# A two-layer kernel on one core: group 0 of the second up stage as seven products, its weight words made during the first stage, and down 1 in another order of products

## The chip, the core and the metric

The kernel runs on one core of a Trainium2 chip. A core has a matrix engine (TensorE, PE in the profile), a vector engine (VectorE, DVE), a scalar engine (ScalarE, ACT), GpSimd (POOL) and a queue engine (SyncE, SP), which issues all the DMAs of this kernel. Matmuls write PSUM, eight banks of 512 fp32 columns by 128 partitions; DVE and ACT read and write PSUM and SBUF. The metric is the device time of one execution in microseconds (us), lower is better. It is compared by medians of several runs.

## What is computed

Attention over small windows (4 batches, 8 heads of 64, 768 positions, chunks of 32 queries) gives x, 3072 tokens by 512. Two feed-forward layers follow, all in fp32:

```
x = attention(q, k, v, mem_k, mem_v)         # 3072 x 512
h = x @ moe_w_in                             # 512 x 2048
g = s * max(h, 0)**2 + b
x = g @ moe_w_out                            # 2048 x 512
h = x @ moe2_w_in
g = h - tanh(h)
out = g @ moe2_w_out
```

## The kernel before

**Four stages.** Up 1 (0 to 350.7 us; attention and h of layer 1), down 1 (to 579.9), up 2 (to 819.8), down 2 (to 1052.0). Tokens are the matmuls' columns, 512 a time. Six blocks of 512 tokens make three groups g of 1024. Each fp32 product is three matmuls of reduced operands (`three`, L154 to 157): each operand is split into a high part, copied by ACT, and a low part, the difference, on DVE. The weights come from DRAM as 64-bit words; a 1024-wide piece is rebuilt by ACT (`scaled`, L162) and DVE (`shifted`, L168, and `filled`, L172).

**Seven products.** Both down stages take the 2 x 2 blocks of a matrix product as seven products P1 to P7 of combined blocks instead of eight. The up stages store for each strip of h the seven combinations of its quadrants (`combine`, L443) in DRAM (`o1`, `o2`), and a down stage (class `Down`, L453) loads them as parts. It runs seven passes, one for each product in the order of `ORDER`, of 12 entries (three groups by two halves by two), 12 matmuls an entry. `split(i + 2)` makes the high and low parts two entries ahead of `multiply(i)`. When a group's product is complete, `final1` (L684) adds it to running sums. In down 1 the results are the quadrants X, U, V, Q of the new x, and for groups 1 and 2 also their combinations T1 to T4.

**Up 2.** Eight column strips n of w_in. Group 0 is a plain product: `plain_column` (L948), 12 matmuls, four a strip. Groups 1 and 2 are a `Quad` (L966): seven products of six matmuls in the order P1, P7, P6, P2, P5, P3, P4, the first product of a quad ahead of the end of the one before. ACT copies the running bank out after P1, P6 and P5 (`copy`, L988), DVE adds a second bank (`add`, L991), ACT takes tanh (L995), DVE subtracts (`curve`, through `minus`, L673) and makes the combinations, SP stores them. The strip's weights are rebuilt, split, combined and split again in between (`w2_*`, L793 to 841).

**What sets the order.** The program's order is written out by hand: each engine runs its own instructions in the order in which the code emits them. In up 1 a list of tokens (`START`) orders the first two blocks, then a loop emits each tile t of a block j (L762 to 788): the attention step, the products, `up1_relu` on ACT, `up1_square` on DVE, and at a strip's end the combinations. The attention step (`att_step`, L353) stands on every fourth tile: ACT copies the transposed weights (L314), then `x_high` (L347), later the exponentials (L291). During down 1 the entries carry steps from tables: `WEIGHTS` makes the pass's weights, `READY` loads, scales and fills the w_out words of layer 2 and stores them in DRAM (`wz`), `SUMS` and `SPLITS` make the T operands.

Of the kernel before, what the change touches and what calls it, by code (L numbers as in the profile page):

```python
# [8 lines left out]
F32 = mybir.dt.float32  # L9
# [35 lines left out]
R10 Q14 R11 E10 F18 V9 st2 k3 F17 D10 Q16 X9 K3 r18 T10 r17 Q17 E11 Q18 F19 vv11 r19 C10 Q19 F21 F20  # L45
D11 r20 st3 L9 r21 Q20 V10 k4 K4 T11 X10 F23 F22 L10 r23 Q21 C11 V11 X11 L11 F24 r22 st4 Q23 R12 Q22
vv12 F26 r24 F25 r26 Q24 F27 r25 Q26 k5 K5 Q25 F28 F29 r27 Q27 r28 F30 k6 st5 K6 E12 st6 Q28 r29 F31
# [3 lines left out]
WEIGHTS = {  # L51
# [7 lines left out]
for q in (2, 5, 6):  # L59
    for h in range(2):  # L60
        WEIGHTS[q - 1, 4 * h] = [("sums", q, h), ("high", q, h)]
        WEIGHTS[q - 1, 4 * h + 1] = [("low", q, h)]

READY = {
    (0, 0): [("load", 0, "E7")], (0, 3): [("scale", 0, "E14"), ("load", 1, "E13")], 
    (0, 6): [("fill", 0)], (0, 7): [("load", 2, "E7")], (0, 9): [("scale", 1, "E15")], 
    (1, 0): [("fill", 1)], (1, 1): [("load", 3, "E13")], (1, 2): [("scale", 2, "E14")], 
    (1, 6): [("fill", 2)], (1, 7): [("load", 4, "E7")], (1, 8): [("scale", 3, "E15")], 
    (1, 10): [("fill", 3)], (2, 1): [("scale", 4, "E14")], (2, 10): [("fill", 4)],
    (3, 0): [("load", 5, "E7")], (3, 4): [("scale", 5, "Z9")],  # L70
    (3, 8): [("fill", 5), ("load", 6, "E7")], (4, 2): [("scale", 6, "Z0")],
    (4, 5): [("fill", 6), ("load", 7, "E7")], (4, 8): [("scale", 7, "Z1")],
    (4, 11): [("fill", 7)],
}

SUMS = {(4, 9): [("T3", 1)], (5, 0): [("T3", 2)], (5, 9): [("T1", 1)], (5, 10): [("T2", 1)],
        (6, 1): [("T1", 2)], (6, 2): [("T2", 2)]}

SPLITS = {(5, 6): [("T3", 1)], (6, 5): [("T1", 1)], (6, 9): [("T4", 1)], (6, 10): [("T3", 2)], (6, 11): [("T1", 2)]}

ORDER = ("P1", "P6", "P5", "P7", "P3", "P2", "P4")
# [3 lines left out]
SLOT = {"P1": 0, "P3": 1, "P2": 2, "P5": 3, "P6": 4, "P7": 5, "P4": 6}  # L85


@with_exitstack
def tile_chunk_attention_two_ffn(
# [30 lines left out]
    SIZE = {"E": 2048, "Z": 1024, "Y": 1024, "Q": 1280, "S": 768, "R": 512}  # L120
# [55 lines left out]
    def filled_in_raw(z, raw):  # L176
# [8 lines left out]
    A_RAW = ("E8", "E9")  # L185
    A_QK, A_V = ("Q0", "Q1", "Q2"), ("Z0", "Z1", "Z2")
# [6 lines left out]
    B_S = (("Z2", "Z3"), ("Z4", "Z6"))  # L193
# [3 lines left out]
    B_ACC = {"X": ("Y0", "Y1", "Y2"), "U": ("Y3", "Y4", "Y5"), "V": ("E6", "E6", "Z7")}  # L197
    X2 = {"Q": ("E13", "E14", "E15"), "V": ("E16",),
          "X": (("Z9", "Z10"), ("Z2", "Z3"), ("Z4", "Z6")), "U": ("E7", "E6", ("Z0", "Z1"))}
    B_TMP = ("E16", "E17", "Z8")  # L200
    C_RAW, C_Z, C_W = "E0", "Z5", ("E1", "E10")
    C_OT = (("E4", "E5"), ("E8", "E12"))
    C_T = {("T3", 1): ("Z11", "Y0"), ("T1", 1): "E2", ("T2", 1): "E3", ("T4", 1): "E17",
           ("T3", 2): "E11", ("T1", 2): "E9", ("T2", 2): ("Z8", "Y1"), ("T4", 2): ("Z7", "Y2")}
    C_SHL, C_SNAP = ("Y3", "Y4"), "Y5"
    C_SHL7 = "E0"
    Z2 = {("A11", 0): "Y3", ("A11", 1): "Y4", ("A21", 0): "Z11", ("A21", 1): "Z2",
          ("A22", 0): "Z3", ("A22", 1): "Z8", ("A12", 0): ("E0", 0), ("A12", 1): ("E0", 1)}
    D_WHL = (("E14", "E6"), ("E13", "E16"))
    D_STREAM = ("E1", "E17", "E2", "E9", "E7")  # L210
    D_RING = ("E3", "E11", "E15")
    D_S = (("Z4", "Z6"), ("Z0", "Z1"))
    D_ACC = {"X": ("Z7", "Z5", "Z9"), "U": ("Y0", "Y1", "Y2"), "V": ("E4", "E4", "E12")}
    D_OUT = ("E5", "E8")
# [11 lines left out]
    def make_masks():  # L226
        for nm in ("mid", "first", "last"):
            m = const.tile([P, KE], F32, name=f"mask_{nm}")
# [224 lines left out]
    class Down:  # L453


        def __init__(self, src, zmap, smap, whl, stream, ring, load, view, pick, bias, final, turn, ahead, first):
# [3 lines left out]
            self.later, self.end = [], None  # L460
            self.loaded, self.turn, self.ahead = 0, turn, ahead
            self.parts = [(p, g, h) for p in range(7) for g in (range(NG) if p else first) for h in range(2)]
# [22 lines left out]
        def place_z(self, key):  # L485
            place = self.zmap[key]
            if isinstance(place, tuple):
                if place[1] == 0:
                    self.zt[place[0]] = new(place[0], 2048, F32, "zq")
# [11 lines left out]
        def load_part(self, i):  # L501
            p, g, h = self.parts[i]
            self.part[i] = new(self.stream[i % len(self.stream)], 4 * NB, F32, "part")
            self.load(self.part[i], ORDER[p], g, h)
# [12 lines left out]
        def sums(self, p, half):  # L517

            z = lambda k: self.z[k, half]
            name = ORDER[p]  # L520
# [42 lines left out]
        def split(self, i):  # L563
# [6 lines left out]
            if self.bias is not None and ORDER[p] in ("P1", "P2", "P3", "P6"):  # L570
# [678 lines left out]
```

## Time and profile before

| | us |
|---|---|
| median of 3 runs (lowest, highest) | 1053.42 (1053.35, 1054.23) |
| the profiled execution | 1053.9 |
| its span | 1052.0 |
| PE busy in the span | 1035.1 |
| DVE, ACT busy | 799.4, 529.1 |
| DMA moved | 250.55 MB, 238 GB/s |

The profile is one execution seen by the hardware profiler. A busy time is the sum of an engine's instructions; a matmul's record is longer than the distance to the next one, because they overlap in the pipeline, so that PE's price of a matmul is the distance of two starts. A wait is the idle time before an instruction, put down to the instruction or transfer that released it. A line number is a line of the kernel shown above. The DMA share is the mean busy share of 16 DMA engines.

### The profile page before, as it was taken

The numbers are of one execution on the slowest core, as the hardware profiler recorded it, in microseconds if no ns is written. First come the engines' busy times: TensorE is split into PE (matmuls) and PEld (weight loads), VectorE is DVE, ScalarE is ACT, GpSimd is POOL, SyncE is SP. The second block draws the span as 40 slices with busy tenths as digits, with TensorE's granted clock in tenths as the row PEclk, the third lists the DMA queues.
The fourth block names the chain that finished last, engine by engine and source line by source line (L and its number), as shares of the span: only waits on it lengthen the run. The fifth ranks groups of instructions, "written<-read, shape, count | busy, mean of one in ns | idle before, by whom it ended". The sixth has DMA issues, their size and how long they took to land.

```text
span 1052.0 us, 15226 instructions
## 1 busy us (share of the span) xinstructions
PE 1035.1 (98%) x6000; PEld 858.2 (82%) x6000; DVE 799.4 (76%) x986; ACT 529.1 (50%) x957; POOL 2.7 (0%) x24
## 2 busy tenths in 40 slices
PE   5999999999999999999999999999999999999998
PEld 5788888888888888888888888888888888888887
DVE  7998557777757787888789888877787866766654
ACT  7885354455523565456466543434444554444442
POOL 1000000000000000000000000000000000000000
PEclk9999999999999999999999999999999999999999
DMA  9796378666458998676762365556649985556671
GB/s 324 254 330 240 135 268 299 244 237 218 178 203 323 344 340 307 195 247 243 274 219 103 110 223 198 214 204 231 250 170 372 372 295 194 187 187 232 239 260 61
DMA packets 74279, 250.55 MB, mean 238 GB/s; under 512 B 5600, under 2 KB 5856, under 8 KB 63968
## 3 DMA queue, kind: packets, MB, share of 16 engines
q1 hardware_dynamic: 74208, 249.58, 65.8%
q8 instruction: 47, 0.77, 0.3%
q14 instruction: 24, 0.20, 0.1%
HBM read 151.00 MB, written 98.57 MB: 237 GB/s over the span
## 4 chain that ended last, share of the span: by engine, by line
PE 95%; DMA 3%; DVE 1%; issue 0%; SPq 0%; ACT 0%; ACTq 0%
PE pb L155 30%; PE pb L157 30%; PE pb L156 30%; PE pb L329 2%; PE pb L307 2%; DMA v<-in_vw_dram 2%; PE pb L267 1%; DMA raw<-in_wi_dram 1%; DMA raw<-in_wo_dram 1%; DVE ob L445 0%; SPq L250 0%; DVE ringhringl L572 0%; DVE oa L991 0%; DVE whl L558 0%; ACT ringhringl L571 0%
## 5 line engine op out<-in xcount | busy, mean ns | idle before, releaser
L157 PE MATMUL pb<-ringhringl,whl 128*128 128x512 f32 (+1 forms) x680 | 262.9, 387 | 0.5 <-DVE ringhringl L572 0.5
L156 PE MATMUL pb<-ringhringl,whl 128*128 128x512 f32 (+1 forms) x680 | 262.9, 387 | 0.0
L155 PE MATMUL pb<-ringhringl,whl 128*128 128x512 f32 (+1 forms) x680 | 262.9, 387 | 0.0
L576 ACT ACTIVATE ringhringl<-part 128x1024 fp32r<-128x1024 f32 x120 | 127.3, 1061 | 160.3 <-PE pb L157 154.8
L577 DVE TENSOR_TENSOR ringhringl<-part,ringhringl 128x1024 fp32r<-128x1024 f32 x120 | 146.6, 1223 | 76.7 <-ACT ringhringl L576 76.6
L155 PE MATMUL pb<-xh,w 128*128 128x512 f32 (+1 forms) x392 | 154.0, 393 | 0.0
L157 PE MATMUL pb<-xl,w 128*128 128x512 f32 (+1 forms) x392 | 151.2, 386 | 0.0
L156 PE MATMUL pb<-xh,w 128*128 128x512 f32 (+1 forms) x392 | 151.0, 385 | 0.0
L157 PEld LDWEIGHTS pb<-ringhringl,whl 128*128 128x128 f32 x680 | 127.7, 188 | 26.9 <-DVE ringhringl L572 0.9
L156 PEld LDWEIGHTS pb<-ringhringl,whl 128*128 128x128 f32 x680 | 127.7, 188 | 26.0
L155 PEld LDWEIGHTS pb<-ringhringl,whl 128*128 128x128 f32 x680 | 127.7, 188 | 25.7
L420 ACT ACTIVATE r<-pb 128x512 f32<-128x512 f32 x96 | 55.4, 592 | 108.1 <-PE pb L157 95.3
L430 DVE SCALAR_TENSOR_TENSOR oa<-pb,s_c,r 128x512 f32<-128x512 f32 x96 | 70.6, 746 | 39.9 <-ACT r L420 39.8
L291 ACT ACTIVATE sm<-sm,nmx 128x96 f32<-128x96 f32 x192 | 69.2, 365 | 36.4 <-DVE nmx L285 36.4
L155 PEld LDWEIGHTS pb<-xh,w 128*128 128x128 f32 x392 | 73.6, 188 | 16.1
L157 PEld LDWEIGHTS pb<-xl,w 128*128 128x128 f32 x392 | 73.6, 188 | 15.0
L156 PEld LDWEIGHTS pb<-xh,w 128*128 128x128 f32 x392 | 73.7, 188 | 13.9
L571 ACT ACTIVATE ringhringl<-part,b_c 128x1024 fp32r<-128x1024 f32 x48 | 54.9, 1150 | 39.1 <-PE pb L157 35.6
L572 DVE SCALAR_TENSOR_TENSOR ringhringl<-part,b_c,ringhringl 128x1024 fp32r<-128x1024 f32 x48 | 61.3, 1281 | 13.1 <-ACT ringhringl L571 13.1
L445 DVE TENSOR_TENSOR ob<-oa 128x512 f32<-128x512 f32 x96 | 65.6, 683 | 0.0
L155 PE MATMUL pb<-x2hx2l,w 128*128 128x512 f32 x112 | 43.6, 389 | 0.0
L156 PE MATMUL pb<-x2hx2l,w 128*128 128x512 f32 x112 | 43.6, 389 | 0.0
(209 smaller groups left out, 1441.0 us busy)
## 6 DMA issues: line engine op xcount, KB each, us to landing
o<-ob SPq DMA_DIRECT2D x48, 1024.0 KB, 4.8
part<-o SPq DMA_DIRECT2D x84, 512.0 KB, 4.9
part<-o SPq DMA_DIRECT2D x42, 1024.0 KB, 5.6
o<-oa SPq DMA_DIRECT2D x48, 768.0 KB, 3.6
raw<-in_wi_dram SPq DMA_DIRECT2D x16, 1024.0 KB, 6.5
raw<-in_wo_dram SPq DMA_DIRECT2D x16, 1024.0 KB, 7.9
qk<-in_qk_dram SPq DMA_DIRECT2D x24, 640.0 KB, 7.7
v<-in_vw_dram SPq DMA_DIRECT2D x24, 384.0 KB, 7.2
```

What stands on the lines that cost most here:

```text
L155: nc.tensor.matmul(acc, lhsT=whi, rhs=xhi, start=first, stop=False, skip_group_check=more)
L156: nc.tensor.matmul(acc, lhsT=wlo, rhs=xhi, start=False, stop=False, skip_group_check=more)
L157: nc.tensor.matmul(acc, lhsT=whi, rhs=xlo, start=False, stop=last, skip_group_check=more)
L291: nc.scalar.activation(out=sm[:, h, :], in_=sm[:, h, :], func=AF.Exp, bias=nmx[:, h:h + 1], scale=1.0, accum_out=sums[:, h:h + 1],)
L307: nc.tensor.transpose(out=bank(2 + g)[0:KE, P * r:P * (r + 1)], in_=sm[:, 4 * g + r, :], identity=ident)
L420: nc.scalar.activation(out=r, in_=up_ps[j, t], func=AF.Relu)
L430: nc.vector.scalar_tensor_tensor(out=oab[j, q][0][:, 2 * i:2 * i + 2, k, :], in0=ps2, scalar=s_c[:, 0:1], in1=r2, op0=ALU.mult, op1=ALU.mult,)
L445: sub = lambda o, x, y: eng.tensor_tensor(out=o, in0=x, in1=y, op=ALU.subtract)
L571: nc.scalar.activation(out=xh, in_=src, func=AF.Identity, bias=self.bias)
L572: nc.vector.scalar_tensor_tensor(out=xl, in0=src, scalar=self.bias, in1=xh.bitcast(F32), op0=ALU.add, op1=ALU.subtract)
L576: nc.scalar.activation(out=xh, in_=src, func=AF.Copy)
L577: nc.vector.tensor_tensor(out=xl, in0=src, in1=xh.bitcast(F32), op=ALU.subtract)
```

## The change

Four edits go together.

**Up 2: three groups of seven products.** `plain_column` and `plain_end` are gone. 24 quads, strip by strip, groups 0, 1, 2, run in one loop. A quad's seven products come in the order P6, P2, P5, (next quad's P1), P3, (next quad's P7), P4. The sum add(3) and tanh(3) of the previous quad are emitted ahead of copy(2). The tanh of outputs 1 to 3 goes to PSUM banks 6 and 7, and DVE reads it from there; before, all went to SBUF. The store of a pair is cut 4 and 3 instead of 3 and 4 (`SLOT2`).

```
-    def plain_column(n, i, col):
-        ps = bank2(2 + i)
-        wh, wl = wi[2, n]
-        for c in range(KD):
-            xh, xl = x2_of(c, 1 - col, 0)
-            three(ps[:, col, 0:NB], wh[:, i, c, :], wl[:, i, c, :], xh, xl, c == 0, c == KD - 1)
...
+    for s in range(NQ - 1):
+        q, p, r = quads2[s], quads2[s - 1] if s else None, quads2[s + 1]
+        n, g = q.n, q.g
+        q.mult("P6")
+        if s == 22:
+            q.copy(2)
+        if p:
+            p.add(3)
+            p.tanh(3)
+        if s != 22:
+            q.copy(2)
+        if g == 0:
+            w2_high(n, 3)
+        if p:
+            p.curve(3)
+            p.combo(0)
+        if s == 1:
+            part1("T4", 2)
+        q.mult("P2")
+        q.add(1)
+        if s == 0:
+            part1("T4", 1)
+            part1("=T4", 2)
+            part1("U", 2)
+        if p:
+            p.combos(0)
+            p.combos(1)
...
+        q.mult("P5")
+        q.copy(3)
+        q.tanh(1)
+        q.add(2)
+        q.curve(1)
+        r.mult("P1")
+        r.copy(1)
+        q.tanh(2)
+        q.curve(2)
...
+        q.mult("P3")
+        q.tanh(0)
+        r.mult("P7")
+        q.curve(0)
...
+        q.mult("P4")
...
         def tanh(self, o):
+            if o:
+                src, self.rs[o] = self.out(o), bank(6 + scratch[0] % 2)
+                scratch[0] += 1
+            else:
+                src, self.rs[o] = self.banks[0], self.out(0)
+            nc.scalar.activation(out=self.rs[o], in_=src, func=AF.Tanh)
```

Here is what stands in ACT's order in the middle of up 2, around one strip of before (`keep` and `oa` from `pb` are copies, L988, and tanh of output 0, L995; `ob<-oa` are the other tanh):

```order
L988 ACTIVATE keep<-pb 128x512
L995 ACTIVATE ob<-oa 128x512
L988 ACTIVATE oa<-pb 128x512
L834 ACTIVATE shlh<-z 128x1024
L995 ACTIVATE oa<-pb 128x512
L995 ACTIVATE ob<-oa 128x512 x2
L958 ACTIVATE oa<-pb 128x1024
```

and of after, from one quad's copy(2) to the next one's (L996 copies, L1008 tanh, L894 the high parts of weights):

```order
L996 ACTIVATE keep<-pb 128x512
L996 ACTIVATE oa<-pb 128x512
L1008 ACTIVATE pb<-oa 128x512
L996 ACTIVATE keep<-pb 128x512
L1008 ACTIVATE pb<-oa 128x512
L1008 ACTIVATE oa<-pb 128x512
L894 ACTIVATE w_5583<-words 128x512
L1008 ACTIVATE pb<-oa 128x512
L996 ACTIVATE keep<-pb 128x512
```

Before, the copy to `keep` that frees the running bank stands ahead of the previous output's tanh; after, the last tanh of a quad (`pb<-oa`, next to last row) stands ahead of the next quad's copy(2) (last row). The wide tanh L958 of the plain product is gone.

**Up 1: the words of w_in of layer 2.** For each of the eight strips m the raw words are loaded, scaled, shifted, filled and summed in up 1, and the filled piece and its four combinations are stored in DRAM (`w2z`). Up 2 loads them as 1 MB of ready words and only splits them. Three strips are placed by tokens in `START`, the others by `P2_STEPS` on tiles of the loop.

```
+for m, j, t in ((2, 2, 2), (3, 3, 2), (4, 3, 10), (5, 4, 2), (6, 4, 10), (7, 5, 6)):
+    for step, at in (("load", t - 4), ("scaled", t - 1), ("filled", t), ("sums", t + 2)):
...
+    def p2_scaled(n):
+        p2_z[n] = new("Z5" if n == 1 else "Z6", 1024, F32, "zw")
+        scaled(p2_z[n], p2_raw[n])
...
+    def p2_filled(n):
+        shifted(p2_z[n])
+        filled(p2_z[n], p2_raw[n])
+        nc.sync.dma_start(out=w2z[n][:, 0:1024], in_=p2_z[n])
...
+    def p2_sums(n):
+        z = p2_z.pop(n).rearrange("p (q m) -> p q m", q=4)
...
+        nc.vector.tensor_tensor(out=o[:, 2], in0=z[:, 2], in1=z[:, 3], op=ALU.add)
+        minus(o[:, 0], z[:, 0], z[:, 2])
+        minus(o[:, 1], o[:, 2], z[:, 0])
+        minus(o[:, 3], z[:, 1], o[:, 1])
+        nc.sync.dma_start(out=w2z[n][:, 1024:2048], in_=both)
```

ACT's order in up 1 around an attention step (`pt` are the copies of the transposed weights, `xh` is x_high, `sm` the exponentials), before:

```order
L420 ACTIVATE r<-pb 128x512 x4
L314 ACTIVATE pt<-pb 96x512 x2
L347 ACTIVATE xh<-pb 128x4x128
L291 ACTIVATE sm,sums<-sm,nmx 128x96 x8
L420 ACTIVATE r<-pb 128x512 x3
```

and after:

```order
L444 ACTIVATE r<-pb 128x512 x4
L187 ACTIVATE zw<-raw 128x1024
L338 ACTIVATE pt<-pb 96x512 x2
L371 ACTIVATE xh<-pb 128x4x128
L315 ACTIVATE sm,sums<-sm,nmx 128x96 x8
L444 ACTIVATE r<-pb 128x512 x3
```

The scaled copy of a strip's raw words now stands between the relu and the attention step's copies.

**Down 1: another order and one running sum.** `ORDER1` is P1, P2, P7, P3, P6, P5, P4; one sum W runs through P1, P7, P6, P5, P4, and a second one through P7 and P3. `PARTS` makes and splits X, T3, T2, Q, T1, U, T4 for all three groups as they come, the last ones at the start of up 2. The weights are combined in place (`DownInPlace`).

```
+        if name == "P1":
+            nc.scalar.activation(out=a("W"), in_=ps, func=AF.Copy)
+        elif name == "P2":
+            tt("X", "W", ALU.add)
+        elif name == "P7":
+            nc.scalar.activation(out=a("T3"), in_=ps, func=AF.Copy)
+            tt("W", "W", ALU.add)
+        elif name == "P3":
+            tt("T3", "T3", ALU.subtract)
+        elif name == "P6":
+            tt("W", "W", ALU.add)
+        elif name == "P5":
+            tt("Q", "W", ALU.add)
+        else:
+            tt("W", "W", ALU.subtract)
```

**READY.** The w_out words of layer 2 are loaded earlier; of the table, the last piece:

```
-    (4, 5): [("fill", 6), ("load", 7, "E7")], (4, 8): [("scale", 7, "Z1")],
...
+    (2, 10): [("scale", 5, "Z6")], (3, 0): [("fill", 5)], (3, 1): [("load", 7, "E7"), ("scale", 6, "Z4")],
+    (3, 2): [("fill", 6)], (4, 7): [("scale", 7, "Z6")], (4, 8): [("fill", 7)],
```

SP's order in pass 4 of down 1, before, from the store of one piece of words (`wz`) to the next, with the raw load between (`part` are the loads of operands):

```order
L854 DMA wz_85<-zw 128x1024
L379 DMA raw<-in_wo_dram 128x2048
L662 DMA part<-o_2_75 128x2x512
L662 DMA part<-o_3_76 128x2x512
...
L662 DMA part<-o_4_77 128x2x512
L662 DMA part<-o_5_78 128x2x512
L854 DMA wz_86<-zw 128x1024
```

and after, at the end of pass 2 and the start of pass 3:

```order
L403 DMA raw<-in_wo_dram 128x2048
L712 DMA part<-o_4_77 128x2x512
L712 DMA part<-o_5_78 128x2x512
L869 DMA wz_84<-zw 128x1024
...
L403 DMA raw<-in_wo_dram 128x2048
L869 DMA wz_85<-zw 128x1024
```

Raw loads and stores of words stand closer together, in passes 2 and 3, and the last raw load (the row ahead of `wz_85`) now precedes the store of its own words, `wz_86`, by 20 rows instead of 7.

**Down 2** keeps its seven passes and its order; its first pass takes the parts as (group, half) (0, 0), (1, 0), (2, 0), (0, 1), (1, 1), (2, 1) instead of group by group.

## Rows read from the trace of the kernel before

**Rows 1.** The page, its first line: span and instructions

```profile
span 1052.0 us, 15226 instructions
```

**Rows 2.** Stages: length, busy us (records) by engine, clock, DMA share, GB/s

```profile
0.00:350.70 350.70, 337.65 (x2905) 280.57 (x2905) 257.10 (x399) 189.99 (x580) 2.75 (x24) 1.00 0.71 253
350.70:579.90 229.20, 228.75 (x1009) 189.11 (x1008) 192.16 (x171) 129.66 (x122) 0.00 (x0) 1.00 0.71 247
579.90:819.80 239.90, 239.63 (x1057) 198.12 (x1056) 197.76 (x286) 107.37 (x157) 0.00 (x0) 1.00 0.60 224
819.80:1052.00 232.20, 229.04 (x1033) 190.38 (x1032) 152.39 (x132) 102.08 (x98) 0.00 (x0) 1.00 0.62 222
```

**Rows 3.** Waits of PE, whole span: total us, times, longest

```profile
PE pb L157 <- DVE ringhringl L572: 0.5, 1, 0.5
PE pb L155 <- DVE oa L991: 0.3, 1, 0.3
```

**Rows 4.** Timeline of PE at two gaps: start, duration, line, idle before

```profile
511.40 0.39 PE L156 MATMUL pb<-ringhringl,whl 128*128 128x512 f32 x1
512.25 0.50 PE L157 MATMUL pb<-ringhringl,whl 128*128 128x512 f32 x1 [0.46 <-DVE ringhringl L572]
...
789.14 0.39 PE L157 MATMUL pb<-x2hx2l,shlh 128*128 128x512 f32 x1
789.79 0.50 PE L155 MATMUL pb<-t4h,w 128*128 128x512 f32 x1 [0.27 <-DVE oa L991]
```

**Rows 5.** Waits of ACT, 480 to 520 us: total, times, longest

```profile
ACT zw L162 <- DMA raw<-in_wo_dram: 4.3, 1, 4.3
```

**Rows 6.** Lines of ACT in up 2: count, busy us, mean ns, idle

```profile
L995 ACT ACTIVATE ob<-oa 128x512 f32<-128x512 f32 x48 | 28.4, 623 | 5.7 <-DVE oa L991 5.7
L988 ACT ACTIVATE keep<-pb 128x512 f32<-128x512 f32 x32 | 19.2, 599 | 42.8 <-PE pb L157 42.8
...
L162 ACT ACTIVATE z<-raw 128x1024 f32<-128x1024 f32 x7 | 8.0, 1138 | 1.1 <-DVE shll L673 1.1
```

**Rows 7.** Lines of DVE in up 2

```profile
L673 DVE TENSOR_TENSOR oa<-oa,ob 128x512 f32<-128x512 f32 x48 | 31.5, 686 | 12.1 <-ACT ob L995 11.6
...
L991 DVE TENSOR_TENSOR oa<-keep,pb 128x512 f32<-128x512 f32 x32 | 21.9, 683 | 18.0 <-PE pb L157 18.0
...
L673 DVE TENSOR_TENSOR z<-z 128x256 f32<-128x256 f32 x21 | 8.9, 425 | 0.7
L172 DVE SCALAR_TENSOR_TENSOR z<-raw,z 128x1024 int32<-128x1024 int32 x7 | 8.6, 1226 | 0.2
...
L168 DVE TENSOR_SCALAR z<-z 128x1024 int32<-128x1024 int32 x7 | 4.8, 684 | 0.0
```

**Rows 8.** Timeline in up 2: an ACT copy and the DVE sum behind it

```profile
657.64 0.60 ACT L988 ACTIVATE oa<-pb 128x512 f32<-128x512 f32 x1 [2.12 <-PE pb L157]
...
658.27 0.69 DVE L991 TENSOR_TENSOR oa<-oa,pb 128x512 f32<-128x512 f32 x1 [1.24 <-ACT oa L988]
```

**Rows 9.** Timeline in up 1: ACT, then DVE and PE, at an attention step

```profile
204.25 0.60 ACT L420 ACTIVATE r<-pb 128x512 f32<-128x512 f32 x1 [2.06 <-PE pb L157]
204.75 1.07 ACT L314 ACTIVATE pt<-pb 96x512 f32<-96x512 f32 x2
206.22 0.60 ACT L347 ACTIVATE xh<-pb 128x512 fp32r<-128x512 f32 x1 [0.40 <-PE pb L329]
...
212.50 0.17 DVE L299 TENSOR_SCALAR sums<-sums 128x8 f32<-128x8 f32 x1 [3.04 <-ACT sm L291]
...
213.82 1.40 DVE L430 SCALAR_TENSOR_TENSOR oa<-pb,s_c,r 128x512 f32<-128x512 f32 x2
...
215.22 0.39 PE L155 MATMUL pb<-xh,w 128*128 128x512 f32 x1
```

**Rows 10.** Page, DMA issues: count, KB each, median us from issue to landing

```profile
raw<-in_wi_dram SPq DMA_DIRECT2D x16, 1024.0 KB, 6.5
```

**Rows 11.** One window at the end of up 2, columns as in Rows 2

```profile
790.00:819.80 29.80, 29.80 (x132) 24.67 (x132) 24.18 (x36) 14.03 (x22) 0.00 (x0) 1.00 1.02 388
```

More of the change, by code (lines that the diff above doesn't have):

```diff
@@ new lines @@
+for q in (3, 4, 5, 6):
+    for h in range(2):
+        WEIGHTS1[q - 1, 4 * h] = [("sums", q, h)]
+        WEIGHTS1[q - 1, 4 * h + 1] = [("high", q, h)]
+        WEIGHTS1[q - 1, 4 * h + 2] = [("low", q, h)]
+P2_STEPS = {}
+for m, j, t in ((2, 2, 2), (3, 3, 2), (4, 3, 10), (5, 4, 2), (6, 4, 10), (7, 5, 6)):
+    for step, at in (("load", t - 4), ("scaled", t - 1), ("filled", t), ("sums", t + 2)):
+        if m == 2 and at < 2:
+            continue
+        P2_STEPS.setdefault((j - (at < 0), at % 16), []).append((step, m))
@@ L453, in tile_chunk_attention_two_ffn, with __init__ @@
     class Down:
-        def __init__(self, src, zmap, smap, whl, stream, ring, load, view, pick, bias, final, turn, ahead, first):
+        def __init__(self, src, zmap, smap, whl, stream, ring, load, view, pick, bias, final, turn, ahead,
+                     order, table, parts):
             self.src, self.zmap, self.smap, self.whl, self.stream, self.ring = src, zmap, smap, whl, stream, ring
@@ L635, in run @@
                 p, k = divmod(i, 4 * NG)
-                for step, q, half in WEIGHTS.get((p, k), ()):
+                for step, q, half in self.table.get((p, k), ()):
                     getattr(self, step)(q, half)
@@ L785, in tile_chunk_attention_two_ffn @@
                 down1.split(t - 13)
+            for what, m in P2_STEPS.get((j, t), ()):
+                if what in ("load", "scaled"):
+                    {"load": p2_load, "scaled": p2_scaled}[what](m)
             if i4 == 3 and not (last and q == 3):
@@ L1122, in tile_chunk_attention_two_ffn @@
-    for o in (1, 2, 0):
-        a.curve(o)
-    down2.load_words()
-    down2.load_words()
-    down2.load_part(2)
-    b.mult("P7")
-    a.mult("P4")
-    a.add(3, 2, 1)
-    for half in range(2):
-        down2.sums(0, half)
-        down2.high(0, half)
-    b.mult("P6")
-    b.copy(2)
-    a.tanh(3)
-    a.curve(3)
-    b.begin()
-    b.mult("P2")
-    b.add(1, 1, 2)
-    b.mult("P5")
-    b.copy(3)
-    plain_column(7, 0, 0)
-    a.end()
-    b.add(2, 3, 1)
-    for half in range(2):
-        down2.low(0, half)
@@ L1147, in tile_chunk_attention_two_ffn @@
[L1147 to L1167 removed]
+    down2.end, down2.skip = end2, (3,)
+    NQ = 8 * NG
@@ new lines, in tile_chunk_attention_two_ffn @@
+    quads2 = [Quad(s) for s in range(NQ)]
+    snap.append(new(C_KEEP, 3 * NB, F32, "keep"))
+    q = quads2[0]
+    q.mult("P1")
+    q.copy(1)
+    w2_high(0, 2)
+    q.mult("P7")
+    w2_low(0, 2)
+    for s in range(NQ - 1):
[25 more added lines that the diff above has]
+            p.combos(1)
+        if g == 0:
+            w2_low(n, 3)
+            if n < 7:
+                w2_load(n + 1)
+        if g == 2:
+            w2_high(n + 1, 1)
+        if s == 22:
+            down2.load_part(3)
+            down2.load_words()
+            down2.load_words()
+        q.mult("P5")
[7 more added lines that the diff above has]
+        q.curve(2)
+        if s == 20:
+            down2.load_words()
+            down2.load_words()
+        if s == 21:
+            down2.load_part(1)
+            down2.sums(0, 0)
+            down2.high(0, 0)
+        if s == 22:
+            down2.sums(0, 1)
+            down2.high(0, 1)
+        if g == 2:
+            w2_low(n + 1, 1)
+        q.mult("P3")
+        q.tanh(0)
+        r.mult("P7")
+        q.curve(0)
+        if s == 20:
+            down2.load_part(0)
+        if g == 1 and n < 7:
+            w2_both(n + 1, 0)
+        if g == 2:
+            w2_both(n + 1, 2)
+        if s == 21:
+            down2.low(0, 0)
+        if s == 22:
+            down2.low(0, 1)
+            down2.split(0)
+            down2.load_part(2)
+        q.mult("P4")
```

544 lines of the change are left out of this document (216 added, 328 removed), and 9 rows, old and new, of tables (PARTS, X2).

## The prediction

> **What bounds the kernel now.** I read the stage windows first [rows 2]: PE is busy 337.65 of 350.7 us in up 1, 228.75 of 229.2 in down 1, 239.63 of 239.9 in up 2 and 229.04 of 232.2 in down 2, with the granted clock at 1.00, its 2.4 GHz level, in every stage. DVE and ACT are idle for a fifth to a half of each. So the end is set by the number of matmuls, and an edit elsewhere counts only where it makes PE wait. The second view, PE's waits, says how often that happens: behind the start-up only twice, once for DVE in down 1 and once for DVE in up 2 [rows 3]. On the timeline the starts of neighbouring 512-column matmuls there lie 512.25 - 511.40 = 0.85 us and 789.79 - 789.14 = 0.65 us apart [rows 4]. The undisturbed pitch comes from up 2: 1056 matmuls are in the program, and (239.90 - 0.42) / 1056 = 0.2268 us each [rows 2]. The mean of some 0.39 us of one record is its length in the pipeline, not its price. The two gaps therefore cost 0.62 and 0.42 us. The sum is made against the profiled execution, 1053.9 us (span 1052.0 [rows 1] and 1.9 around it), which lies 0.5 above the median of the runs, 1053.4.
>
> **The change part by part.**
>
> *Fewer matmuls in up 2.* Per column strip n, group 0 took two strips by two columns by four chunks by three = 48 matmuls; as seven products of two chunks by three it takes 42. Eight strips: 48 matmuls fewer, 1056 to 1008. All other stages keep their matmul counts. 48 x 0.2268 = **-10.9 us**, since PE is the bound and dense here.
>
> *The two gaps.* The one at 512 us began with ACT waiting 4.3 us for a raw weight load [rows 5], in front of a split for PE; that load stood three entries ahead of its use. In the new READY table the last load stands at (3, 1) and its use at (4, 7), 18 entries (49 us) later. The one at 790 us came from DVE finishing a pair sum behind a strip's combinations, an order that no longer exists. Together **-1.0 us**, and 0 if others like them open.
>
> *Each quad in up 2.* With seven products the 24 quads are all alike, 7 x 6 x 0.2268 = 9.53 us of PE each. I laid out one quad by hand from its P6 at T, with 0.60 us for an ACT copy, 0.62 for a tanh [rows 6], 0.69 for a 512-wide DVE sum [rows 7], and a hand-over of 0.03 (the copy ends at 658.24, DVE starts at 658.27) [rows 8]. The previous quad's add(3) runs from 0.20 to 0.89, its tanh(3) from 0.92 to 1.54; only behind it in ACT's queue comes copy(2), which has to empty the bank before P5, but whose own product P6 ends only at 1.53. It runs 1.57 to 2.17, and PE wants the bank at 2.72: 0.55 us to spare. The copy before P3 ends at 4.89 against 5.45, also 0.56. DVE has 11 operations of 512 in every quad and at most two more (the lows of the next weights, in group 2): 13 x 0.686 = 8.9 us [rows 7], under 9.53, though with its waits for tanh(3) and for P2 it is done only at about 9.35 where the next add(3) can begin at 9.73. I take **0**. What covers it is those 0.55 us; without them each microsecond late per quad costs 24.
>
> The tanh of outputs 1 to 3 now writes a PSUM bank and DVE reads it there. No row has ACT writing PSUM. The nearest are a tanh from SBUF to SBUF, 623 ns, and a copy from PSUM to SBUF, 599 ns [rows 6]; I take 0.62, with 0.60 to 1.2 (twice) as bounds. For DVE the rows do compare: the sum with one operand in PSUM took 683 ns and the one from SBUF alone 686 [rows 7]. [...]
>
> *The first quads.* At the start of up 2 no previous quad fills DVE, but three 1024-wide operations do (T4 of group 1, its subtraction for group 2, the split of U 2), 3 x 1.22 us, then one more split. Add(2) of quad 0 then ends within 0.1 us of P4's need. Between 0 and 0.6 us; I take **+0.3**.
>
> *Up 1 makes the words.* Eight times: a 1 MB load, a scaled copy on ACT (1.14 us) [rows 6], on DVE a shift, a fill and four quarter sums (0.68 + 1.23 + 4 x 0.425 = 3.6 us) [rows 7], two stores of 0.5 MB. DVE rises from 257 to 286 of 350.7 us, ACT from 190 to 199 [rows 2]: no bound by sums. By place: shift and fill fall into DVE's wait for the exponentials, 3.04 us long [rows 9]. The scaled copy stands right before an attention step's copies in four places. There relu ended at 204.85, the copies ran 204.75 to 205.82, and x_high began at 206.22 waiting for PE [rows 9]; 1.14 us put in front moves x_high by about 0.53 us. This runs on through the mask and the exponentials to the square, the first of the two at 213.82, ending near 214.57; PE wanted its bank at 215.22 [rows 9]. 0.65 - 0.53 = 0.12 us left. The quarter sums take a similar room. Bounds: 0, and 0.25 us at each of eight places, 2.0. I take **+0.3**. The load is issued three tiles and one attention step ahead of its use: 3 x 12 x 0.2268 = 8.2 us of products and the step's own matmuls, against 6.5 to landing [rows 10]. That is covered by 2 us or a little more; the SP queue issues these loads behind stores that wait for DVE, and what comes later than that stands on ACT in front of PE's relus.
>
> *Down 1.* Same matmuls in another order; three of the 21 sums on DVE become copies on ACT, three more operands are split, and the making of strip 0's weights (3.6 us of DVE) goes. DVE's 192 of 229 us [rows 2] stay about that, and none of the seven passes of 12 x 2.72 = 32.7 us is full: **0**. Between (2, 5) and (3, 2), 24.5 us, the queue gets 4.5 parts and three raw loads of 1.05 MB and four stores of 0.52 MB: 10.0 MB, or 407 GB/s. The highest long window of the trace is 388 GB/s at a DMA share of 1.02 [rows 11]; at that the burst is 25.7 us long, 1.2 late. ACT's earlier wait of 4.3 us [rows 5] reached PE with 0.62, so about 3.7 us are free there: 0. [...]
>
> *Boundary to down 2.* Its first part order changes so that only groups already finished are asked for early; the last part's load waits for the last strip's stores as it did, and by my count is there when its split comes up, some 5 us before PE wants it: 0.
>
> **Sum:** 1053.9 - 10.9 - 1.0 + 0.3 + 0.3 = 1042.6 in a profiled run, 0.5 less against the median: **1042.1 us**.
>
> **The rivals.**
> *A: the chain add(3), tanh(3), copy(2) is late in every quad.* For it: copy(2) now queues behind a tanh that waits for DVE, and the room is 0.55 us, 0.4 on DVE. Against it: every duration in it has a row but one. A lateness at P5 of 0.1 to 0.3 us a quad costs 24 times that, 2.4 to 7.2: 1044.5 to 1049.3.
> *B: up 1 stalls.* The words' loads land late, or the shifted attention chain lacks more than its 0.12 us: six places by 0.2 to 1 us, 1.2 to 6: 1043 to 1048.
> *C: DMA saturates in down 1's burst, or where up 1 ends.* One or two waits beyond the 3.7 us that are free: 0.5 to 4 us, 1042.6 to 1046.
> *D: slower than before.* One mechanism: DVE does not keep a quad's pace. If ACT's write to PSUM took twice as long, 1.2 us, tanh(3) would end at 2.1 and copy(2) at 2.8, 0.1 beyond need, and DVE, waiting for three such results, would pass 9.53 us a quad. Each quad is then DVE's length. From 0.57 us a quad on (13.6 us in 24) the 11.4 are gone and 2.1 more: 1055.5 and above.
> *E: the gain is hidden.* Another engine sets up 2, so that 48 matmuls fewer end in waits: 1051.5 to 1055. Against it: DVE is busy 197.8 of 239.9 us there now [rows 2], and its work per strip stays about equal.
>
> **How the numbers follow.** Forecast (1041.3 to 1043.3) 0.55, A 0.16, B 0.13, C 0.08, D 0.04, E 0.04. A difference of 0.2%, 2.1 us, is about what a measurement of this kernel can tell from no change. Faster: forecast, A, B and C, 0.92. Same: E, 0.04. Slower: D, 0.04. The low end is the forecast without its two additions and 0.5 less, 1041.0. The high end, 1047.0, takes in C and the larger halves of A and B.
>
> **What would show it.** After the change: up 2 has some 1008 matmul records in about 229 us, with PE without gaps; no PE wait for DVE near down 1's middle; PE's waits in up 1 as before. Right for the forecast is PE at 99% of the last three stages. A: PE waits for ACT's keep copies (L996), about 24 times. B: PE waits in up 1 for a square, or ACT for raw weight words. C: ACT waits for zw or parts in down 1. I'm wrong if PE is dense but its pitch is above 0.2268 us, which nothing here would explain.

## The result

| | before | after |
|---|---|---|
| median of the runs taken together (lowest, highest), us | 1053.83 (1053.35, 1056.31) | 1040.66 (1040.41, 1045.06) |
| the profiled execution, its span | 1053.9, 1052.0 | 1040.41, 1038.6 |
| ratio, 95% interval | | 0.988 (0.985 to 0.9911) |

The changed kernel is 13.2 us faster by these medians, 1.2%. The forecast was 1042.1, 11.3 less than before; the time lies 0.3 us below the low end of the range, 1041.0. The direction is right, and so is the size of what the change did: the stages account for 11.1 to 11.8 of the 13.2 us, and the rest lies in the start and was luck, as shown below. The steps can be checked one by one, because the stages behind the first 100 us take the same time in every profile of a kernel to 0.1 us, but for one stage of one profile. What the forecast did not see is that the first 40 us of either kernel vary by about 3 us.

The page and the stage windows of the changed kernel, columns as in [rows 2]:

```profile
span 1038.6 us, 15266 instructions
...
PE 1026.1 (99%) x5952; PEld 850.5 (82%) x5952; DVE 817.1 (79%) x1043; ACT 551.9 (53%) x1019; POOL 2.7 (0%) x24
```

```profile
0.00:349.50 349.50, 340.12 (x2905) 281.80 (x2906) 281.80 (x447) 197.98 (x588) 2.74 (x24) 0.99 0.83 299
349.50:577.95 228.45, 228.45 (x1009) 189.16 (x1008) 192.32 (x169) 135.32 (x129) 0.00 (x0) 1.00 0.71 247
577.95:806.10 228.15, 228.15 (x1008) 188.83 (x1007) 186.70 (x289) 115.91 (x202) 0.00 (x0) 1.00 0.60 232
806.10:1038.60 232.50, 229.40 (x1035) 190.69 (x1033) 156.28 (x140) 102.68 (x100) 0.00 (x0) 1.00 0.64 229
```

Against [rows 2]: up 2 has 1008 matmul records in 228.15 us where there were 1056 in 239.90, and PE is busy in all of it. Down 1 is 0.8 us shorter, with PE busy throughout. DVE's load in up 1 rose from 257 to 282 us and the DMA share from 0.71 to 0.83, and PE shows almost nothing of it. PE is still the bound: 99% of the span, DVE 79%, ACT 53%.

PE's waits over the whole span of the changed kernel; the columns are total us, times, longest:

```profile
PE pb L291 <- DMA qk<-in_qk_dram: 4.8, 1, 4.8
PE pb L331 <- DVE sm L325: 3.5, 2, 2.3
PE pb L353 <- issue: 0.4, 1, 0.4
PE pb L353 <- DVE w L424: 0.4, 1, 0.4
```

All four lie in the first 30 us. The two waits of [rows 3] are gone and none came in their place.

Since the start varies, I compare stages from the start times of matmuls read from the timelines: the 1000th matmul record (counted from 0; in up 1, at about 87 us), the first of down 1, the first of up 2 and the last of all. Five profiles of the two programs (one with an edit that concerns the start alone, below):

| profile | 1000th matmul at | to down 1 | down 1 | up 2 and down 2 |
|---|---|---|---|---|
| before | 87.01 | 263.69 | 229.23 | 468.63 |
| before again | 89.95 | 263.69 | 228.48 | 468.63 |
| before, masks in the side pool | 85.97 | 263.76 | 228.48 | 468.66 |
| after | 85.48 | 263.99 | 228.48 | 457.27 |
| after again | 88.44 | 263.98 | 228.48 | 457.22 |

The rest of this document is about this table: -11.4 in up 2, +0.3 in up 1, -0.75 or 0 in down 1, and a first column that differs by 3 us within one and the same program. Four of the experiments below, with one run each, took 1043.72 to 1044.41 us in all; their 1000th matmul started at 88.8 to 89.6 us, so that only their stages can be compared. The order of down 1, the PSUM places of the tanh and the cut of the stores were not tried by themselves.

### The profile page after: what moved, and what is told of

It reads as the page before. It is cut to its first block, busy times and chain, and to the rows that moved or that the text cites. A ratio compares the mean times of both kernels' runs of the same rounds, so it can differ in the third digit from the quotient of the medians.

```text
span 1038.6 us, 15266 instructions
## 1 busy us (share of the span) xinstructions
PE 1026.1 (99%) x5952; PEld 850.5 (82%) x5952; DVE 817.1 (79%) x1043; ACT 551.9 (53%) x1019; POOL 2.7 (0%) x24
## 4 chain that ended last, share of the span: by engine, by line
PE 97%; ACT 2%; DVE 1%; DMA 0%; issue 0%; DVEq 0%
PE pb L180 31%; PE pb L182 30%; PE pb L181 30%; PE pb L353 2%; PE pb L331 2%; PE pb L291 1%; ACT sm L315 1%; DMA qk<-in_qk_dram 0%; ACT pt L338 0%; DVE sm L302 0%; DVE xl L375 0%; DVE w L424 0%; ACT z L187 0%; DVE nmx L309 0%; ACT xh L371 0%
## 5 line engine op out<-in xcount | busy, mean ns | idle before, releaser
L180 PE MATMUL pb<-x2hx2l,w 128*128 128x512 f32 x224 | 87.2, 389 | 0.0
L181 PE MATMUL pb<-x2hx2l,w 128*128 128x512 f32 x224 | 87.2, 389 | 0.0
L182 PE MATMUL pb<-x2hx2l,w 128*128 128x512 f32 x224 | 87.1, 389 | 0.0
L1008 ACT ACTIVATE pb<-oa 128x512 f32<-128x512 f32 x72 | 43.2, 599 | 53.8 <-DVE oa L1000 52.9
```

What stands on the lines that cost most here:

```text
L180: nc.tensor.matmul(acc, lhsT=whi, rhs=xhi, start=first, stop=False, skip_group_check=more)
L181: nc.tensor.matmul(acc, lhsT=wlo, rhs=xhi, start=False, stop=False, skip_group_check=more)
L182: nc.tensor.matmul(acc, lhsT=whi, rhs=xlo, start=False, stop=last, skip_group_check=more)
L1008: nc.scalar.activation(out=self.rs[o], in_=src, func=AF.Tanh)
```

## The experiments

**Six matmuls more in every strip.** P1 of group 0 is multiplied twice.

```
     q = quads2[0]
+    q.mult("P1")
     q.mult("P1")
...
         r.mult("P1")
+        if r.g == 0:
+            r.mult("P1")
```

> The changed kernel with P1 of group 0 multiplied twice in every strip (the second time overwrites the same bank with the same values): six more matmuls per strip, 48 in all, as many as the change removed. Theory 1 (PE is the bound in up 2 and each matmul costs its pitch): 48 x 0.2268 = 10.9 us more than the changed kernel, about 1051.5, with PE still free of gaps. Rival (the gain came from elsewhere, from the order or from the second engines, and PE has room): clearly less than 10.9, under 5.

Measured: 1054.09 us as the median of ten runs (1051.54 to 1055.43), ratio to the kernel before 0.9995 (0.9981 to 1.0009): the gain is gone. The stages tell it more sharply: up 2 and down 2 take 468.11 us instead of 457.27, 10.84 more for 48 matmuls, 0.226 each, without a gap. The 0.5 us that remain to the kernel before's 468.63 are its gap at 790 us. So the gain in up 2 is the price of 48 matmuls and of that gap; the new order adds nothing of its own.

**Six matmuls fewer in every quad.** Half of P2 and half of P4 are left out.

```
-            for c in range(2):
-                three(acc, wh[:, c], wl[:, c], xh[:, c], xl[:, c], c == 0 and new_, c == 1, not new_)
+            cs = (0,) if name in ("P2", "P4") else (0, 1)
+            for c in cs:
+                three(acc, wh[:, c], wl[:, c], xh[:, c], xl[:, c], c == 0 and new_, c == cs[-1], not new_)
```

> The changed kernel with the second half (three matmuls) of P2 and of P4 left out in each of the 24 quads, so that the result lacks these terms: 36 matmuls a quad, 8.16 us of PE instead of 9.53. It measures how far DVE and ACT are from setting up 2. By the hand-laid quad DVE is done at about 9.35 in quads of group 2 and at about 8.6 in the others, some of it waits that shrink along with PE. Theory 1: PE gains nearly all of 24 x 1.361 = 32.7 us, 28 to 32, and first stalls appear in front of P6 or P5 in group 2 alone. Rival (DVE or ACT is close behind PE in all quads): less than 25 us gained, stalls in all 24.

Measured: up 2 and down 2 took 442.87 us, 14.4 less than the changed kernel's 457.27, not 28 to 32. PE's waits behind 100 us, then up 2 as a window (from 1.06 us ahead of its first matmul):

```profile
PE pb L180 <- ACT keep L997: 8.7, 16, 1.2
PE pb L180 <- DVE oa L1001: 0.9, 2, 0.5
```

```profile
579.90:797.60 217.70, 208.07 (x881) 162.87 (x880) 186.00 (x292) 114.89 (x204) 0.00 (x0) 1.00 0.63 246
```

My expectation was wrong here and the rival nearer, though neither fits: PE waits 18 times, not 24, 16 of them for the copy to `keep`, and not for a full engine (DVE is busy 186 of 217.7 us). A strip of three quads settles at 26.3 us, by the starts of corresponding stalls (657.99, 684.28, 710.51), where PE alone would need 24.5 and the changed kernel takes 28.6. What PE waits for is the chain add(3), tanh(3), copy(2). At one of a strip's two stalls add(3) stands behind operations of DVE that follow each other without a pause, at the other behind a low part of weights that had waited 0.55 us for ACT (at 681.78 us). With these matmuls left out a strip needs 26.3 us. The change therefore used room that was there, and something like 2 us a strip are left: 2.3 by these stalls, 1.8 as an eighth of the 14.4 us, since the first quads and one later strip lost more. That is an estimate for matmuls of P2 and P4; leaving out others was not tried.

**Tanh(3) three times.** By estimate 1.04 us more on ACT in front of copy(2).

```
             p.add(3)
             p.tanh(3)
+            p.tanh(3)
+            p.tanh(3)
```

> The changed kernel with tanh(3) of the previous quad issued three times (twice for nothing) ahead of copy(2): about 2 x 0.52 = 1.04 us more on ACT in the tightest link of a quad. Theory 1 (copy(2) has 0.55 us to spare before P5): 1.04 - 0.57 = 0.47 us a quad in 22 quads, 10 us slower than the changed kernel, with PE waiting for ACT keep once a quad, a little more if DVE, which waits for the same tanh, passes its own room. Rival (the true room is 1 us or more, or PE is held by something else): no more than 2 us slower.

Measured: up 2 and down 2 took 470.00 us, 12.7 more, and the whole 1057.93. PE waited for `keep` in nearly every quad; the waits, and one of the stalls on PE's timeline:

```profile
PE pb L180 <- ACT keep L996: 5.9, 21, 0.9
```

```profile
658.76 0.39 PE L182 MATMUL pb<-x2hx2l,w 128*128 128x512 f32 x1
659.39 0.50 PE L180 MATMUL pb<-x2hx2l,w 128*128 128x512 f32 x1 [0.25 <-ACT keep L996]
659.73 0.39 PE L181 MATMUL pb<-x2hx2l,w 128*128 128x512 f32 x1
```

The starts are 0.63 to 0.64 us apart where 0.23 is the pitch: 0.41 late, against 0.47 by the hand-laid quad. The next start is 0.34 behind, 0.11 more than the pitch, so that a stall costs 0.52 here. Most stalls are of this size, the first two larger. The tightest link of the schedule is the one the prediction named, and its room was sized to 0.06 us.

**Copy(2) ahead of add(3) and tanh(3).**

```
-        if s == 22:
-            q.copy(2)
+        q.copy(2)
         if p:
             p.add(3)
             p.tanh(3)
-        if s != 22:
-            q.copy(2)
```

> The changed kernel with copy(2) ahead of the previous quad's add(3) and tanh(3) in every quad, as only quad 22 has it. Theory 1 (the order costs nothing, since copy(2) has 0.55 us to spare): the time of the changed kernel within 0.3 us in up 2. Rival (the order protects another link: curve(3) and DVE behind it come 0.6 us later and stall PE): 2 us or more slower.

Measured: up 2 and down 2 took 457.79 us, 0.5 more, with a single gap of 0.64 us between starts, at 599.54 in the second quad, ahead of its P3. PE waited there for copy(3), which by the profile had itself waited for DVE's split of T4, a leftover of down 1. The order is free in the steady state and costs half a microsecond at the beginning. This is between my 0.3 and the rival's 2; with the order of the changed kernel the first quads lost nothing.

**Word-making left out, or moved.** Once the words of strips 3 to 7 are not made in up 1; once their scaled copy stands one tile earlier.

```
-for m, j, t in ((2, 2, 2), (3, 3, 2), (4, 3, 10), (5, 4, 2), (6, 4, 10), (7, 5, 6)):
+for m, j, t in ((2, 2, 2),):
...
-        nc.sync.dma_start(out=words[n], in_=w2z[n])
+        nc.sync.dma_start(out=words[n], in_=w2z[n % 3])
```

> The changed kernel with the word-making of strips 3 to 7 left out of up 1, and up 2 loading the words of strips 0 to 2 in their place (wrong weights, same work in up 2). It leaves out 5 loads, 5 scaled copies, 5 shifts and fills and 20 quarter sums. Theory 1 (the scaled copy in front of an attention step overruns its 0.12 us of room by less than 0.1): up 1 is 0.2 to 0.4 us shorter, and the short delays of PE after the four attention steps are gone. Rival (the additions cost up 1 by DVE's or DMA's load as a whole): 1 us or more shorter.

```
-    for step, at in (("load", t - 4), ("scaled", t - 1), ("filled", t), ("sums", t + 2)):
+    for step, at in (("load", t - 4), ("scaled", t - 2), ("filled", t), ("sums", t + 2)):
```

> The changed kernel with the scaled copy of the words in the up 1 loop one tile earlier (two tiles ahead of its fill instead of one), so that it no longer stands right ahead of an attention step's copies. Theory 1 (that place overran its room by under 0.1 us four times): from the 1000th matmul to down 1 it takes 263.7 us, as in the kernel before, instead of 264.0. Rival (the raw load then lands too late and ACT waits): PE waits behind ACT in up 1 and it takes 264.5 us or more.

Measured from the 1000th matmul to down 1: 263.76 us without the words, 263.76 with the copy moved, 263.99 in the changed kernel, 263.69 before. Both times 0.23 us come back. Set side by side matmul by matmul, the changed kernel falls behind at three of the four places, by about 0.08 us each, and keeps up at the fourth, where no exponentials follow. Here is the first of them in the changed kernel, ACT then PE, to be read beside [rows 9]:

```profile
203.20 1.16 ACT L187 ACTIVATE zw<-raw 128x1024 f32<-128x1024 f32 x1
204.26 1.07 ACT L338 ACTIVATE pt<-pb 96x512 f32<-96x512 f32 x2
205.21 0.61 ACT L371 ACTIVATE xh<-pb 128x512 fp32r<-128x512 f32 x1
```

```profile
213.46 0.39 PE L182 MATMUL pb<-xl,w 128*128 128x512 f32 x1
213.69 0.44 PE L180 MATMUL pb<-xh,w 128*128 128x512 f32 x1
213.97 0.39 PE L181 MATMUL pb<-xh,w 128*128 128x512 f32 x1
```

The scaled copy pushes x_high behind the end of the values; it starts right behind the other copies instead of waiting 0.40 us for PE. Counted from the 1000th matmul it is 0.52 us later than in [rows 9], where the prediction had 0.53. Eight microseconds later the square frees its bank late, and what waits for the bank is the weight load (PEld) that runs ahead of the matmul. Here is that load before and after, then all such waits of the changed kernel between 100 and 349 us (total us, times, longest):

```profile
215.00 0.19 PEld L155 LDWEIGHTS pb<-xh,w 128*128 128x128 f32 x1
```

```profile
213.63 0.19 PEld L180 LDWEIGHTS pb<-xh,w 128*128 128x128 f32 x1 [0.20 <-DVE oa L454]
```

```profile
PEld pb L180 <- DVE oa L454: 0.6, 3, 0.2
```

Before, the load starts 0.22 us ahead of its matmul at 215.22; after, it comes 0.16 late by the count from the 1000th matmul. PE's distance of two starts is 0.28 once instead of 0.23, and smaller ones behind it bring the delay to 0.08. The kernel before has no wait of this kind there. The 5 MB of loads and 5 MB of stores and DVE's 18 us do not show in PE at all.

**The last raw load late.** In the changed kernel it is moved to one entry ahead of its use.

```
-    (2, 10): [("scale", 5, "Z6")], (3, 0): [("fill", 5)], (3, 1): [("load", 7, "E7"), ("scale", 6, "Z4")],
+    (2, 10): [("scale", 5, "Z6")], (3, 0): [("fill", 5)], (3, 1): [("scale", 6, "Z4")], (4, 6): [("load", 7, "E7")],
```

> The changed kernel with the last raw load of w_out words in down 1 moved from (3, 1) to (4, 6), one entry (2.7 us) ahead of its scaled copy. It brings back the wait that the kernel before had in down 1 (4.3 us of ACT, 0.73 us of PE with the weight load behind it). Theory 1 (ACT has some 3.6 us of room ahead of PE there): the load lands 5 to 8 us after its issue, ACT waits 3 to 5.5 us and PE loses 0 to 2 us, one gap in down 1. Rival (the gap of the kernel before had another cause): no gap in spite of a wait of 4 us or more.

Measured: down 1 took 228.52 us, 0.04 more, although ACT waited for raw words in it for 3.6 us at once (total us, times, longest):

```profile
ACT zw L187 <- DMA raw<-in_wo_dram: 5.1, 2, 3.6
```

The wait stayed under the rival's 4 us, so that this run alone does not decide between the two; the profiles of the next experiment do.

**The kernel before once more, and with its identity and masks in the side pool.** The side pool is where the changed kernel keeps them; of the edits it is the one that touches what the first microseconds use.

```
-    ident = const.tile([P, P], F32, name="ident")
+    ident = side["of"].tile([P, P], F32, tag="ident", name="ident")
...
-            m = const.tile([P, KE], F32, name=f"mask_{nm}")
+            m = side["of"].tile([P, KE], F32, tag=f"mask_{nm}", name=f"mask_{nm}")
```

> The kernel before once more, unchanged, for a second profile of its start-up. Theory 1 (scatter): its 300th matmul starts at another time than 32.25 us, by several tenths. Rival (the start-up is fixed by the program): within 0.1 us of 32.25.

> The kernel before with the identity and the three masks allocated in the side pool, as the changed kernel has them, and nothing else. In the first 30 us the changed kernel is about 1.5 us ahead of the kernel before, though the instructions there are the same. Theory 1 (scatter of the first transfers from run to run): the start-up gain is not tied to this edit; the 300th matmul starts anywhere between 30.5 and 32.5 us. Rival (the new places in SBUF speed up the start): it starts near 30.7, as in the changed kernel, and the whole is 1.5 us under the kernel before.

Measured: 1056.1 us and 1052.21 us, one run each. The 1000th matmul started at 89.95 and 85.97 us. (The mark that the expectations call the 300th matmul, at 32.25 us in the first profile of before, is record 400 by the count used here; it started at 34.60 and 31.22 us.) The unchanged program alone covers 87.01 to 89.95, the changed one 85.48 to 88.44 (and other kernels with its start up to 90.3). So the start is not fixed by the program. Whether the side pool makes an early start likelier, one run of it can't tell; it took 1.0 us less than the run of before beside it, 1053.23. In both, down 1 took 228.48 us, without the gap at 512 us, and ACT's wait for the raw words was shorter than the 4.3 us of [rows 5]; of before again:

```profile
ACT zw L162 <- DMA raw<-in_wo_dram: 3.0, 1, 3.0
```

Waits of 2.8 (side pool), 3.0 and 3.6 us cost PE nothing or 0.04, and one of 4.3 cost 0.75. ACT's room there is about 3.6 us, close to the 3.7 that the prediction had worked out; but the gap was an accident of one execution. How many of the runs without a profile had it isn't known.

**The first products ahead of the waiting values.** In the start-up list V3, which waits for a load, goes behind G1, which does not need it.

```
-V3 z1 G1 i1 S7 X2 X3 G0 L2 o1 L3 h1 l1 E4 F0 ra2 M7 F1 D4 z2 R7 F2 E6 T4 r0 qk8 i2 r1 h2 S8 o2 ra3
+z1 G1 V3 i1 S7 X2 X3 G0 L2 o1 L3 h1 l1 E4 F0 ra2 M7 F1 D4 z2 R7 F2 E6 T4 r0 qk8 i2 r1 h2 S8 o2 ra3
```

> The changed kernel with the first half of products G1 on PE ahead of values V3 in the start-up list, instead of behind it. In ten profiles PE waited 0.4 to 2.7 us for the v load in front of V3, G1 needs only tokens 0 and 1 and the first weights, and where that wait was long the granted clock fell to its lower level in the next 6 us. Theory 1 (the scatter of the runs is made by this wait and the clock behind it): the products of G1 fill the wait, the 1000th matmul starts at 85.0 to 87.0 us instead of 85.5 to 90.3, and the median is 1 to 3 us under the changed kernel's in the same session. Rival (the scatter is made by the DMAs before, and PE only waits at the next place): the same median within 0.5 us and the same scatter.

> The changed kernel once more, unchanged, to see its scatter in the session of the run before. Theory 1 (scatter of the start-up alone): times between 1040.4 and 1045.5 us in two or three clusters, while the stages from the 1000th matmul to the last take 949.7 us within 0.2. Rival (the scatter lies in the changed stages): other lengths behind the 1000th matmul.

> The changed kernel with both small edits: G1 ahead of V3 in the start-up list, and the scaled copies of the words one tile earlier. Theory 1: behind the 1000th matmul 949.5 us instead of 949.7, the 1000th matmul at 85.0 to 87.0 us, and a median of 1040.5 to 1041.5, against 1040.66 and 1042.83 of the changed kernel in its two sessions. Rival (the start-up's scatter is not in V3's wait): a median above 1042.

Measured: G1 first 1041.1 us (1040.8 to 1043.55, four runs), the changed kernel beside it 1042.83 (1040.65 to 1043.31), both edits 1041.63 (1040.96 to 1042.73). The 1000th matmul started at 86.45 and 86.67 with G1 first and at 88.44 in the changed kernel's second profile. Behind it, all three took what was expected: 949.72, 949.68 and 949.46 us. The first median lies 1.7 us under the changed kernel's beside it, as expected, the third 0.1 above its range. For the start the result is inconclusive: eight runs with G1 first (four of them with both edits) have a median of 1041.4, the changed kernel's eight 1041.6, and the ranges overlap. The expectation's "where that wait was long the granted clock fell" has an exception among its ten profiles, the first one of before, with a wait of 2.29 us and a clock of 1.00. The scatter seems narrower (1040.8 to 1043.55 against 1040.41 to 1045.06), and a new wait of 0.4 us for DVE at about 41 us takes a part back. Neither edit is shown to beat the changed kernel; its up 1 part, 0.23 us, is below what the medians can tell.

## Why the prediction was right, and what it missed

*The matmuls.* Forecast 48 x 0.2268 = 10.9, measured 10.84 by putting 48 back. Right.

*The two gaps.* The one at 790 us was in every profile of the kernel before (0.65 to 0.66 between starts) and is gone. The forecast priced a gap by its one long distance, 0.42; the next start is late as well, 0.34 instead of 0.23, as in the timeline of the third experiment, so that it cost 0.53: 468.63 - 457.27 = 11.36 is 10.84 + 0.52. The gap at 512 us, 0.75 with its own late start, was taken for a part of the kernel and was an accident of that execution, absent in two others. In the table the change of READY is worth 0.75 against the profiled execution and 0 against the others. The step that failed is this second gap's 0.62 us: a single wait of 4.3 us at the edge of a room of 3.6 should have been given a chance, not counted in full.

*Each quad.* Forecast: copy(2) from 1.57 to 2.17 behind T, PE needing the bank at 2.72. Here is a quad of group 0 in the changed kernel, DVE, ACT and PE; its P6 starts at T = 694.99, P5 at 697.71:

```profile
695.18 0.69 DVE L1000 TENSOR_TENSOR oa<-keep,pb 128x512 f32<-128x512 f32 x1 [0.41 <-PE pb L182]
```

```profile
695.91 0.60 ACT L1008 ACTIVATE pb<-oa 128x512 f32<-128x512 f32 x1 [2.33 <-DVE oa L1000]
696.54 0.60 ACT L996 ACTIVATE keep<-pb 128x512 f32<-128x512 f32 x1
```

```profile
694.99 0.39 PE L180 MATMUL pb<-x2h,w 128*128 128x512 f32 x1
...
697.71 0.39 PE L180 MATMUL pb<-x2hx2l,w 128*128 128x512 f32 x1
```

Add(3) begins at T + 0.19, tanh(3) at 0.92, copy(2) runs 1.55 to 2.15, P5 starts at 2.72. All within 0.02 us of the hand layout. DVE was idle for 0.41 us ahead of that add(3); the forecast had 0.38 for the quad behind one of group 2. In 22 of the 23 quads of the loop copy(2) lies there to 0.01 us; in the third it runs 1.89 to 2.47, still ahead of P5. Rivals A and D are out (D's bound adds up to 1055.8 rather than 1055.5, which changes nothing), and so is E, by the six matmuls more. How near A was: 0.57 us a quad by these lines, about 0.6 by the experiment with tanh(3).

On DVE another quad is tighter than the one that was laid out. In a quad behind one of group 1 (T = 656.91) a low part of the next weights, which waits for ACT, ends just as add(3) can begin:

```profile
656.41 0.69 DVE L721 TENSOR_TENSOR w<-words,w 128x512 fp32r<-128x512 f32 x1 [0.70 <-ACT w L894]
657.11 0.69 DVE L1000 TENSOR_TENSOR oa<-keep,pb 128x512 f32<-128x512 f32 x1
```

Add(3) is not late here, but this is where the second kind of stall in the experiment with fewer matmuls arose.

The one duration without a row came out at the low bound. ACT's tanh into PSUM, and DVE's difference with an operand there, lines of up 2 (count, busy us, mean ns, idle):

```profile
L1008 ACT ACTIVATE pb<-oa 128x512 f32<-128x512 f32 x71 | 42.6, 599 | 53.1 <-DVE oa L1000 52.9
```

```profile
L721 DVE TENSOR_TENSOR oa<-oa,pb 128x512 f32<-128x512 f32 x69 | 47.3, 686 | 17.6 <-ACT pb L1008 15.8
```

The tanh took 599 ns where it took 623 into SBUF [rows 6], 24 ns less. DVE took 686 ns with the operand in PSUM, as it had with both in SBUF [rows 7]; going by the row was right.

*The first quads.* Forecast +0.3, measured 0: after the gap and the matmuls nothing of the 11.36 us is left for it. The bound of 0 was the truth; three 1024-wide operations of DVE fitted.

*Up 1.* Forecast +0.3, measured +0.23 to 0.3, in the place named (the attention steps' squares), and gone in both experiments on it. The 0.12 us of room were counted to the matmul's start; the weight load wants the bank 0.22 earlier, so that there was no room and the squares held PE up a little. Place and mechanism were right; the 0.3 was a choice between 0 and 2.0, and that it came out so closely was luck. Rival B is out.

*Down 1, boundary.* Forecast 0, measured 0: 228.48 us in both programs where the raw load came in time. Rival C is out, with ACT's room of 3.6 us used at no place of the changed kernel (its longest wait for raw words in down 1 is 1.0 us).

*What was missing: the start.* Behind the 1000th matmul the profiled executions differ by 961.55 - 949.74 = 11.8 us, and against the kernel before in its other profiles by 11.1. The forecast's own terms make 11.3. The other 1.5 us of the profiled pair are in the first column of the table. They are no gain of the change: the kernel with six more matmuls a strip has the changed kernel's start and 960.56 us behind the 1000th matmul, 0.2 to 1.0 less than the profiles of before, and its ten runs have a median 0.1 us under before's, 1054.09 against 1054.17. That the changed kernel's first four runs came out under the range is luck of the start; over its eight runs the median is 1041.6. Here are windows from 28 to 30 and from 30 to 36 us, of after, of before again and of the first profile of before:

```profile
28.00:30.00 2.00, 2.00 (x40) 1.93 (x40) 2.00 (x4) 1.32 (x3) 0.00 (x0) 1.00 0.56 141
30.00:36.00 6.00, 6.00 (x75) 5.75 (x74) 5.93 (x10) 5.64 (x24) 0.00 (x0) 1.00 0.94 351
```

```profile
28.00:30.00 2.00, 0.38 (x7) 0.41 (x9) 1.68 (x4) 1.60 (x2) 0.00 (x0) 0.76 0.43 109
30.00:36.00 6.00, 6.00 (x75) 5.44 (x73) 3.54 (x5) 4.37 (x19) 0.00 (x0) 0.51 0.75 282
```

```profile
28.00:30.00 2.00, 0.60 (x20) 0.63 (x22) 1.58 (x3) 1.57 (x2) 0.00 (x0) 1.00 0.64 126
30.00:36.00 6.00, 6.00 (x88) 5.68 (x85) 5.20 (x9) 5.41 (x20) 0.00 (x0) 1.00 0.86 323
```

In the first, the load for V3 landed at 27.76 us, PE was busy from 28 to 30 and the granted clock was 1.00 there and in the 6 us behind. In the second it landed at 29.48, PE was busy for 0.38 of these 2 us, and the granted clock was 0.51 in the 6 us behind. The load's landing and the clock behind it together moved the 1000th matmul by 4.5 us between these two. The third pair of windows takes them apart: before's first profile waited as long (2.29 us against 2.31, until 29.40 and 29.62), its clock stayed at 1.00, and its 1000th matmul started 2.94 us earlier than in before again. The later end of the wait makes 0.2 us of that; the rest goes with the clock. The prediction took the three runs of before, which spread by 0.9 us, for the scatter of the kernel; over the 32 runs of before in all sessions it is 1052.03 to 1056.42. A range for a time of four runs had to hold that.

## What to carry to other kernels

Where one engine is busy 98% of the span, count its instructions first: 48 matmuls at their start-to-start pitch gave the gain to 1%, and a hand-laid schedule of the waiting engines, made only of durations and hand-overs from rows, told to some hundredths of a microsecond that nothing would eat it. A single gap in one execution is not a property of the kernel; see whether a second profile has it, or how far the wait behind it stands from the room. Compare stages between marks inside the program, so that a start-up that varies does not enter.

## What the runs showed of the hardware

Behind a stall the second start came late as well: that matmul began 0.34 us later instead of 0.23, at both gaps of the kernel before (512.25 and 789.79 us) and at the stall of the third experiment shown above (659.39 us). In up 1 a bank that came free late was waited for by the weight load, for 0.20 us at 213.63 us; in the kernel before that load had started 0.22 us ahead of its matmul. The views give the granted clock as a share. At 1.00, matmuls of 512 columns started 0.2268 us apart and those of 256 columns 0.12 (changed kernel, from 1034.62 us on): 256 columns more took 0.107 us, 2.4 columns a ns, and in this sense the prediction's 2.4 GHz. While matmuls ran, every window read with a granted clock well below 1.00 lies in the first 40 us, down to 0.50 in the kernel before again (30 to 34 us); behind 30 us eight of the fourteen profiles have such windows, six with a mean of 0.69 to 0.86 from 30 to 40 us and two with 0.50 and 0.61 from 30 to 32. In the first profile of before, PE was busy only 0.60 of the 2 us from 28 to 30 and the clock was 1.00 in the next 6 us, in the second one of after it was busy 0.58 and the clock's mean in the next 6 us was 0.72. What decides between these two stays open.
